# The tail of an attention and top-8 MLP kernel: full-height gather matmuls, bf16 broadcasts, one tile's statistics on ScalarE, other wait and hint places

## The chip, the cores and the metric

The kernel runs on one core of a Trainium2 chip. Its engines are TensorE (PE in the profile; its weight loads are PEld), VectorE (DVE), ScalarE (ACT), GpSimd (POOL) and SyncE (SP), which issues most of the DMAs. Each engine has its own in-order instruction stream, and they meet through semaphores. The metric is device time in microseconds, the median over several executions.

## The reference

For x of 2048 rows by 448 columns, in bf16:

```
h  = x + Attn(layernorm(x))          # 16 heads of 28 columns, one K and one V for all heads
n  = layernorm(h)
r  = n @ w_r                         # one score per row
idx = the 8 rows with the largest r
y  = ((silu(n[idx] @ w_gate) * (n[idx] @ w_up)) @ w_down) * sigmoid(r[idx])
out = h + n, with y added to the 8 rows idx
```

The gate and up matrices are 448 by 1792, the down matrix 1792 by 448. Only 8 rows go through the MLP, but which 8 they are is known only when r of all 2048 rows is known.

## The kernel before, in words

**Planner.** The kernel describes its work as a list of operations, each with its engine, an estimated duration, the keys that it reads and writes, and a priority (`_Graph.op`). `plan` simulates the five engines with these estimates and picks, whenever an engine is free, the ready operation with the lowest priority number. What comes out is a fixed order for each engine. `finish` works out which semaphore waits remain, and `emit` (L217) writes the instructions: of the waits of one instruction, the last in the list is carried by the instruction itself, and those ahead of it become waits of their own in front of it; a DMA gets all of them in front.

**Attention.** The work is 16 blocks: block b takes head group b % 4 (4 heads) and query quarter b // 4 (512 queries). A block goes over 16 key tiles of 128 keys. For most tiles ScalarE takes the exponential of two 128x1024 score tiles (`act_unit`, L884); for three to five of them VectorE builds it by integer arithmetic (`dve_unit`, L896, and `shift`, L902). TensorE multiplies the result with V into an accumulator bank. After a block (`post_block`) the sums are inverted and the block's output is scaled, on POOL and by way of DRAM; for the last block, b = 15, this is done at once on VectorE and ScalarE: a shuffle that copies the row sums to all rows (L640), a clamp (L642), Ln and Exp as reciprocal (L646, L648), each in two halves of 256 columns, and four products of 128 columns (L652).

**The last four row tiles.** Tiles 0 to 11 are projected, normalised and written out during the attention. For tiles 12 to 15 `last_pre` accumulates the first three head groups and the residual in PSUM banks 3 to 6 beforehand. What follows block 15 is one dependent chain, the tail:

- `last_proj` adds the fourth head group (one matmul per tile) and takes mean and variance of each tile on VectorE (L810, L811).
- `last_ln` takes 1/sqrt(variance) by Ln and Exp on ScalarE (L816, L818), forms r of the 512 rows on VectorE (L820 to L827; L827 writes it to a spare column of `x_sb`), and has ScalarE write the normalised rows `xn` (L836). The reciprocals `Li` of the last block's row sums (L662) stand in VectorE's order among these; they only feed a range flag.
- r is turned into a row by four matmuls (L1010), and VectorE finds the 8 largest of 8 earlier candidates and 512 new values (L1012, L1013).
- The 8 positions are cast to f32 (L1015) and broadcast to all 128 partitions by an f32 matmul with a 1-row column of ones (L1021). Comparing them with a row index gives one-hot columns `oh5` (L1023): four blocks of 128 rows for the tiles, and a fifth, 8 rows high, for candidates from earlier tiles, whose rows lie in `xnc` and `extc` (8 partitions).
- The weights 1/(1+exp(-r)) are computed (L1016 to L1020) and broadcast by a second f32 matmul (L1027, copied out by L1029).
- The gather (L1036 to L1041): for each of four column chunks, four matmuls with 128 rows and one with 8 rows pick the 8 rows of n into `xselT` (L1042). Five small matmuls give the row numbers for the scatter (L1054 to L1059).
- Gate and up projections are 56 matmuls each (L1066); silu is Exp, Ln, Exp on ScalarE, the first reading PSUM (L1071), then three VectorE products (L1074 to L1079), in two halves.
- `row_mm` (L1044) gathers h + n of the 8 rows by the same 4 + 1 matmuls per chunk, into the banks in which the 56 down-projection matmuls (L1084) then accumulate. The sum is copied out (L1088), transposed back, cast (L1093, L1095), and scattered to 8 rows of the output by an indirect DMA on POOL (L1096).

**Branch at the end.** Each engine reads the range flag (L1141) and branches (L1152) past a second, exact version of the kernel that follows in its stream; a branch hint instruction (L1137) stands in the middle of each engine's order. SP then waits for the output DMAs (L1168).

Nearly all tensors are touched through two helpers: matmuls have L371 (in the changed kernel L383), DMA issues of SP L385.

## Time and profile before

| | |
|---|---|
| median of 3 runs | 404.59 us (404.42 to 405.1) |
| profiled execution: its own time | 403.72 us |
| profiled execution: span of the core | 401.9 us |
| ScalarE busy | 375.6 us (93%) |
| VectorE busy | 354.8 us (88%) |
| TensorE busy | 348.9 us (87%) |
| GpSimd busy | 62.2 us (15%) |
| last ScalarE exponential of the attention ends | 377.87 us |
| last instruction that computes (scatter issue on POOL) ends | 399.07 us |

The span is the time from the first to the last instruction in the trace; the execution's own time contains in addition what lies around it. Busy shares are averages over the whole span; the tail is the last 24 us of it and has its own limits, so it is read by the timeline, instruction by instruction. A timeline row gives start, length, engine, line, operation, tile names and sizes, the number of merged instructions, and in brackets how long the engine had been idle and who released it.

### The profile page before, as it was taken

Reading aid. Unit: us, or ns where it says so; the run is one execution under the profiler, and the core shown is the slowest. Engines: PE = TensorE matmul, PEld = TensorE weight load, DVE = VectorE, ACT = ScalarE, POOL = GpSimd, SP = SyncE. Lnnn points to the kernel's source line nnn. Section 1 sums busy time; section 2 is a strip of 40 time slices with the busy share of each in tenths; the row PEclk is TensorE's granted clock in tenths of the full one; section 3 lists DMA queues with packets and bytes.
Section 4 is the critical chain, followed back from the end, with each engine's and each line's share of the span. In section 5 each row is a group of like instructions: output and inputs, shape, how many; then the busy total and the mean of one; then the engine's idle time right before and its main releaser. Section 6 shows DMA issues by size and latency. Waiting matters only on the chain.

```text
span 401.9 us, 8036 instructions
## 1 busy us (share of the span) xinstructions
PE 348.9 (87%) x3367; PEld 109.9 (27%) x3367; DVE 354.8 (88%) x577; ACT 375.6 (93%) x423; POOL 62.2 (15%) x111
## 2 busy tenths in 40 slices
PE   7899889898897989989898989899898989789854
PEld 7333222222222222222222222222222222222244
DVE  6995799998899999898999899998989999999361
ACT  4999999999999999999999999999999999999761
POOL 8240001211001021101011111111020121206000
PEclk9999999999999999999999999999999999999955
DMA  7694000100010010110001000200001110111010
GB/s 195 175 246 148 1 2 3 56 3 27 2 31 0 6 48 3 42 36 27 25 29 47 22 31 5 72 2 29 27 27 47 44 44 19 49 46 32 1 43 14
DMA packets 18078, 17.14 MB, mean 43 GB/s; under 512 B 6684, under 2 KB 15156, under 8 KB 18036
## 3 DMA queue, kind: packets, MB, share of 16 engines
q1 hardware_dynamic: 17940, 16.55, 14.1%
q8 instruction: 27, 0.44, 0.5%
q14 instruction: 15, 0.12, 0.1%
q0 software_dynamic: 96, 0.03, 0.1%
HBM read 11.71 MB, written 4.86 MB: 41 GB/s over the span
## 4 chain that ended last, share of the span: by engine, by line
ACT 62%; PE 17%; DVE 17%; POOL 1%; issue 1%; DMA 1%; SPq 1%; POOLq 0%; DVEq 0%
ACT P L884 61%; PE ps L371 17%; DVE Y L896 7%; DVE Y L902 5%; DMA wv_sb<-in_A_wv_dram 1%; POOL hbuf L702 1%; SPq L385 1%; DVE Ot L658 1%; DVE bn L810 1%; DVE junk L710 0%; DVE hbuf L696 0%; DVE x_sb L708 0%; DVE Q L488 0%; DVE wo_pad L784 0%; DVE bn L698 0%
## 5 line engine op out<-in xcount | busy, mean ns | idle before, releaser
L884 ACT ACTIVATE P<-ps 128x1024 bf16<-128x1024 f32 x390 | 361.9, 1083 | 5.1 <-PE ps L371 3.9
L371 PE MATMUL ps<-Q,K 64*128 64x512 bf16 x1024 | 180.7, 384 | 35.9 <-ACT P L884 27.8
L896 DVE TENSOR_SCALAR Y<-ps 128x1024 int16<-128x1024 f32 x122 | 148.1, 1214 | 15.3 <-PE ps L371 15.1
L902 DVE TENSOR_SCALAR Y<-Y 128x2048 int16<-128x2048 int16 x122 | 119.1, 976 | 2.1
L371 PEld LDWEIGHTS ps<-Q,K 64*128 64x128 bf16 x1024 | 44.5, 93 | 179.1 <-ACT P L884 143.3
L371 PE MATMUL ps<-Y,Vs 128*32 128x512 bf16 x976 | 84.8, 383 | 2.9 <-DVE Y L902 2.9
L371 PE MATMUL ps<-P,Vs 128*32 128x512 bf16 x780 | 77.2, 388 | 0.0
L670 POOL TENSOR_TENSOR Ls<-Ls,Lc 128x16 f32<-128x16 f32 x15 | 9.9, 661 | 188.7 <-DMA Lc<-h_scr 188.7
L371 PEld LDWEIGHTS ps<-Y,Vs 128*32 128x32 bf16 x976 | 24.6, 95 | 32.4 <-issue 16.8
L371 PEld LDWEIGHTS ps<-P,Vs 128*32 128x32 bf16 x780 | 19.8, 93 | 43.2 <-issue 42.1
L674 POOL TENSOR_TENSOR On<-Ot,Rb 128x512 bf16<-128x512 f32 x15 | 19.2, 1283 | 76.7 <-DMA Rb<-h_scr 76.7
L371 PE MATMUL ps<-xnT,wq_pad 112*128 112x512 bf16 (+1 forms) x68 | 19.4, 371 | 0.4 <-DVE Ot L658 0.2
L371 PE MATMUL ps<-wo_pad,On 128*128 128x448 bf16 (+1 forms) x64 | 17.2, 358 | 1.5 <-DVE On L652 1.5
L702 POOL TENSOR_TENSOR hbuf<-st,nhalf 128x1 f32<-128x1 f32 x12 | 9.5, 791 | 20.2 <-DVE st L700 20.2
L488 DVE TENSOR_SCALAR Q<-ps,qone 128x512 bf16<-128x512 f32 x15 | 10.8, 717 | 1.1 <-PE ps L371 1.1
L658 DVE COPY Ot<-ps 128x512 f32<-128x512 f32 x15 | 10.2, 680 | 0.0
L710 DVE SCALAR_TENSOR_TENSOR junk<-hbuf,w_rb 128x448 bf16<-128x448 f32 x12 | 8.1, 677 | 0.0
L696 DVE TENSOR_TENSOR hbuf<-ps,x_sb 128x448 f32<-128x448 f32 x12 | 7.4, 618 | 0.8 <-PE ps L371 0.8
L371 PE MATMUL ps<-ident 128*128 128x128 bf16 x72 | 6.2, 253 | 1.8 <-POOL ident L400 1.8
L698 DVE BATCH_NORM_STATS2 bn<-hbuf 128x6 f32<-128x448 f32 x12 | 7.4, 617 | 0.1
L589 DVE BATCH_NORM_STATS2 bn<-x_sb 128x6 f32<-128x448 bf16 x12 | 7.0, 604 | 0.0
L371 PEld LDWEIGHTS ps<-wo_pad,On 128*128 128x128 bf16 x64 | 4.2, 97 | 9.5 <-issue 5.8
(185 smaller groups left out, 162.0 us busy)
## 6 DMA issues: line engine op xcount, KB each, us to landing
Rb<-h_scr SPq DMA_DIRECT2D x15, 256.0 KB
h_scr<-hbuf SPq DMA_DIRECT2D x12, 225.0 KB, 2.4
out_dram<-x_sb SPq DMA_DIRECT2D x8, 224.0 KB, 2.2
wg_sb<-in_B_w_gate_dram SPq DMA_DIRECT2D x1, 1568.0 KB, 11.4
wu_sb<-in_B_w_up_dram SPq DMA_DIRECT2D x1, 1568.0 KB, 17.7
wd_sb<-in_B_w_down_dram SPq DMA_DIRECT2D x1, 1568.0 KB, 21.0
x_sb<-in_A_x_dram SPq DMA_DIRECT2D x3, 448.0 KB, 5.6
x_sb<-in_A_x_dram SPq DMA_DIRECT2D x4, 112.0 KB, 2.3
```

The lines of the kernel that those rows point to most:

```text
L371: return lambda e: e.matmul(o, lhsT=l, rhs=r, start=start, stop=stop)
L488: G.op(DV, lambda e: e.tensor_scalar(Q[:, b % 4, :], ps[:, bank, :], qone[:, 0:1], None, ALU.add), dvt(512), reads=[pk(bank), "qone"], wri ...
L658: G.op(DV, lambda e: e.tensor_copy(Ot[:, rb, :], ps[:, acc_bank(b), :]), dvt(512), reads=[pk(acc_bank(b))], writes=[("Ot", rb)], prio=u - 30)
L670: G.op(LE, lambda e: e.tensor_tensor(Ls[:, :], Ls[:, :], Lc[:, rb, :], ALU.add), 150, reads=["Ls", ("Lc", rb)], writes=["Ls"])
L674: G.op(PO, lambda e: e.tensor_tensor(On[:, qb % 2, g, :], Ot[:, rb, :], Rb[:, rb, :], ALU.mult), 1270, reads=[("Ot", rb), ("Rb", rb)], wri ...
L696: G.op(DV, lambda e: e.tensor_tensor(h, ps[:, bank, 0:D], x_sb[:, t, 0:D], ALU.add), dvt(D), reads=[pk(bank), ("x", t)], writes=[("h", hr)])
L698: G.op(DV, lambda e: e.bn_stats(bn6[:, t, :], h), dvt(D), reads=[("h", hr)], writes=[("bn6", t)])
L702: G.op(PO, lambda e: e.tensor_tensor(s4, st[:, t, 7:8], nhalf[:, 0:1], ALU.pow), 570, reads=[("st7", t), "nhalf"], writes=[("h4", hr)])
L710: G.op(DV, lambda e: e.scalar_tensor_tensor(junk[:, :], h, s4, w_rb[:, :], ALU.mult, ALU.mult, accum_out=st[:, t, 2:3]), 700, reads=[("h", ...
L884: G.op(AC, lambda e: e.activation(P[:, sl, :, :], ps[:, b0:b0 + 2, :], ACT.Exp, bias=EBIAS, scale=OCT), 905, reads=[pk(b0), pk(b0 + 1)], w ...
L896: G.op(DV, lambda e: e.tensor_scalar(Y[:, n, 0, p:p + 3:2, :].bitcast(I16), ps[:, 4:6, :], 0.0, 32639.0 - 3 * STEP, ALU.max, ALU.min), 114 ...
L902: G.op(DV, lambda e: e.tensor_scalar(Y[:, n, v:2 * v, :, :].bitcast(I16), Y[:, n, 0:v, :, :].bitcast(I16), v * STEP, None, ALU.add), 70 + ...
```

## The change

The list below follows the diff from top to bottom.

1. **Waits sorted.** `emit` sorts an instruction's waits by the time at which the planner expects them to be met, latest last. `op` gets an argument `after`, an order without a semaphore.
2. **Full height.** `extc` and `xnc` become 128 partitions high; the region is cleared once by POOL (`clear_ext`), which the built order places on POOL between the sixth `Ls` and the sixth `Lsi`. The fifth matmul of each gather then has 128 rows.
3. **Constants.** POOL fills a bf16 128x128 tile of ones and a cleared bf16 128x5x8 tile `bz` at the start.
4. **Last block.** The halves are taken one after the other: shuffle, clamp, shuffle, clamp on VectorE; Ln, Exp, Ln, Exp on ScalarE.
5. **Statistics.** Tile 12's mean and variance come from two ScalarE passes over PSUM with summed outputs (Identity, then Square about the mean) and one small VectorE scaling; the three other tiles stay on VectorE. In the built order the flag's `Li`, `Ls` come after the three `ra` operations, and `Lsi` after r.
6. **Position broadcast.** The positions are split in two bf16 terms (a cast and a subtraction) in row 0 of `bz` and broadcast by two bf16 matmuls of 128 rows.
7. **Weights.** They are computed later (ScalarE takes their Exp after the fourth `xn`), split in three bf16 terms by four more VectorE operations, and broadcast by three bf16 matmuls into bank 7; in the built order these stand between the gate and the up projection.
8. **Silu.** VectorE first copies the gate to SBUF, clamped at -43, for each half; the Exp reads that copy.
9. **Hints.** On POOL and SP the branch hint stands first in the order, ahead of SP's first load. VectorE's flag load moves, in the built order, from behind `idxc` to between the last `guT` product and the copy `yT`.

```diff
     def op(self, eng, fns, dur, reads=(), ..., form=0,
+           after=()):
...
+        for p in after:
+            need(p, p.eng != eng)
...
+    def met(self, wait):
+        key, v = wait
+        o = self.ops[key[1]] if isinstance(key, tuple) else self.orders[key][v - 1]
+        return o.end + o.lat
...
-            for key, v in self.waits[o.idx].items():
+            for key, v in sorted(self.waits[o.idx].items(), key=self.met):
...
-    extc = xnF[0:8, 3072:3072 + XW + 16]
-    xnc = xnF[0:8, 3584:3584 + D + 16]
+    extc = xnF[:, 3072:3072 + XW + 16]
+    xnc = xnF[:, 3584:3584 + D + 16]
...
+    G.op(PO, lambda e: e.memset(onesb[:, :], 1.0), 200, writes=["onesb"])
+    G.op(PO, lambda e: e.memset(bz[:, :, :], 0.0), 100, writes=["bz"])
...
+    def clear_ext():
+        G.op(PO, lambda e: e.memset(xnF[:, 3072:4096], 0.0), 1100, writes=xk(1))
...
+        if k == 0:
+            G.op(AC, lambda e: e.activation(hbuf[:, 0, 0:D], ps[:, bank, 0:D], ACT.Identity, scale=1.0 / D,
+                                            accum_out=mv[:, t, 0:1]), 650, reads=[pk(bank)], writes=[("h", 0), ("mv0", t)])
+            G.op(AC, lambda e: e.activation(hbuf[:, 0, 0:D], ps[:, bank, 0:D], ACT.Square, bias=mv[:, t, 0:1],
+                                            scale=-1.0, accum_out=sq[:, 0:1]), 650,
+                 reads=[pk(bank), ("mv0", t)], writes=[("h", 0), "sq"])
+            G.op(DV, lambda e: e.tensor_scalar(mv[:, t, 1:2], sq[:, 0:1], 1.0 / D, None, ALU.mult), 70,
+                 reads=["sq", ("mv0", t)], writes=[("mv", t)], prio=301)
+            return
...
-    G.op(DV, lambda e: e.tensor_copy(posf[:, 1, :], idx8[:, 1, :]), 90, ...)
-    G.op(PE, mm(ps[:, 2, 0:8], ones1[:, :], posf[:, 1, :], True, True), 100, ...)
+    G.op(DV, lambda e: e.tensor_copy(bz[0:1, 0, :], idx8[:, 1, :]), 90, reads=[("idx8", 1), "bz"], writes=["bz0"])
+    G.op(DV, lambda e: e.tensor_tensor(bz[0:1, 1, :], idx8[:, 1, :], bz[0:1, 0, :], ALU.subtract), 90, ...)
+    G.op(PE, [mm(ps[:, 2, 0:8], onesb[:, :], bz[:, i, :], i == 0, i == 1) for i in range(2)], 60, ...)
...
-    G.op(PE, mm(ps[:, 2, 8:16], ones1[:, :], wrow[:, :], True, True), 100, reads=["ones1", "wrow"],
-         writes=[pk(2)], prio=310.5)
...
-        fns.append(mm(psg[:, ch, :], xnc[:, ch * CK:ch * CK + 128], oh5[0:8, 4, :], False, True))
+        fns.append(mm(psg[:, ch, :], xnc[:, ch * CK:ch * CK + 128], oh5[:, 4, :], False, True))
...
+    G.op(PE, [mm(ps[:, 7, 64:72], onesb[:, :], bz[:, i, :], i == 2, i == 4) for i in range(2, 5)], 90,
+         reads=["onesb", "bz", "bz2", "bz3", "bz4"], writes=[pk(7)], prio=321.5)
...
-        fns.append(mm(psy[:, ch, :], extc[:, ch * CK:ch * CK + 128], oh5[0:8, 4, :], False, False))
+        fns.append(mm(psy[:, ch, :], extc[:, ch * CK:ch * CK + 128], oh5[:, 4, :], False, False))
...
+        G.op(DV, lambda e, sl=sl, bg=bg: e.tensor_scalar(eg[:, sl, :], pgu[:, bg, :, :], -43.0, None, ALU.max), 130, ...)
...
-                at = {lst[len(lst) // 2].idx: [hint]}
+                at = {lst[0 if eng in (PO, SP) else len(lst) // 2].idx: [hint]}
```

More of the change, by code (lines that the diff above doesn't have):

```diff
@@ L1014, in _main @@
          writes=[("idx8", 1)])
-    G.op(DV, lambda e: e.tensor_copy(posf[:, 1, :], idx8[:, 1, :]), 90, reads=[("idx8", 1)], writes=[("posf", 1)])
-    G.op(AC, lambda e: e.activation(wrow[:, :], top8[:, 1, :], ACT.Exp, scale=-1.0), 200, reads=[("top8", 1)],
-         writes=["wrow"])
-    G.op(DV, lambda e: e.tensor_scalar(wrow[:, :], wrow[:, :], 1.0, None, ALU.add), 70, reads=["wrow"],
-         writes=["wrow"], prio=311)
-    G.op(DV, lambda e: e.reciprocal(wrow[:, :], wrow[:, :]), 100, reads=["wrow"], writes=["wrow"], prio=311)
-    G.op(PE, mm(ps[:, 2, 0:8], ones1[:, :], posf[:, 1, :], True, True), 100, reads=["ones1", ("posf", 1)],
-         writes=[pk(2)])
+    G.op(DV, lambda e: e.tensor_copy(bz[0:1, 0, :], idx8[:, 1, :]), 90, reads=[("idx8", 1), "bz"], writes=["bz0"])
+    G.op(DV, lambda e: e.tensor_tensor(bz[0:1, 1, :], idx8[:, 1, :], bz[0:1, 0, :], ALU.subtract), 90,
+         reads=[("idx8", 1), "bz0"], writes=["bz1"])
+    G.op(PE, [mm(ps[:, 2, 0:8], onesb[:, :], bz[:, i, :], i == 0, i == 1) for i in range(2)], 60,
+         reads=["onesb", "bz", "bz0", "bz1"], writes=[pk(2)])
     G.op(DV, lambda e: e.tensor_tensor(
@@ L1026, in _main @@
         writes=["oh5"])
-    G.op(PE, mm(ps[:, 2, 8:16], ones1[:, :], wrow[:, :], True, True), 100, reads=["ones1", "wrow"],
-         writes=[pk(2)], prio=310.5)
-    G.op(DV, lambda e: e.tensor_copy(wbc[:, :], ps[:, 2, 8:16]), 70, reads=[pk(2)], writes=["wbc"], prio=330)
+    G.prio = 321
+    G.op(AC, lambda e: e.activation(wrow[:, :], top8[:, 1, :], ACT.Exp, scale=-1.0), 200, reads=[("top8", 1)],
+         writes=["wrow"])
+    G.op(DV, lambda e: e.tensor_scalar(wrow[:, :], wrow[:, :], 1.0, None, ALU.add), 70, reads=["wrow"],
+         writes=["wrow"])
+    G.op(DV, lambda e: e.reciprocal(wrow[:, :], wrow[:, :]), 100, reads=["wrow"], writes=["wrow"])
+    G.op(DV, lambda e: e.tensor_copy(bz[0:1, 2, :], wrow[:, :]), 90, reads=["wrow", "bz"], writes=["bz2"])
+    G.op(DV, lambda e: e.tensor_tensor(wlo[:, :], wrow[:, :], bz[0:1, 2, :], ALU.subtract), 90, reads=["wrow", "bz2"],
+         writes=["wlo"])
+    G.op(DV, lambda e: e.tensor_copy(bz[0:1, 3, :], wlo[:, :]), 90, reads=["wlo", "bz"], writes=["bz3"])
+    G.op(DV, lambda e: e.tensor_tensor(bz[0:1, 4, :], wlo[:, :], bz[0:1, 3, :], ALU.subtract), 90, reads=["wlo", "bz3"],
+         writes=["bz4"])
     for k in range(4):
```

45 lines of the change are left out of this document (28 added, 17 removed).

## Prediction

> **What bounds the kernel now.** I read the page first (slices, chain, groups), then the timeline of the last 24 us, instruction by instruction.
>
> ```profile
> span 401.9 us, 8036 instructions
> PEclk9999999999999999999999999999999999999955
> ACT 62%; PE 17%; DVE 17%; POOL 1%; issue 1%; DMA 1%; SPq 1%; POOLq 0%; DVEq 0%
> L884 ACT ACTIVATE P<-ps 128x1024 bf16<-128x1024 f32 x390 | 361.9, 1083 | 5.1 <-PE ps L371 3.9
> ```
>
> ScalarE carries the chain: 390 exponentials, 361.9 of 401.9 us, with 5.1 us idle before them in all. The instruction order of the attention is the same in both kernels apart from one POOL memset and the hints, so that part keeps its time. Behind them comes the tail, where no engine is full and one dependent chain sets the end. The granted clock is 0.5 in the last two slices (381.8 on), so the matmul rows from there on are at that clock already.
>
> The tail's timeline (start, length, engine, line):
>
> ```profile
> 379.31 0.48 DVE L642 TENSOR_SCALAR Ot<-Ot 128x256 f32<-128x256 f32 x2
> 380.25 0.70 ACT L648 ACTIVATE Rb<-Rb 128x256 f32<-128x256 f32 x2
> 380.68 0.88 DVE L652 TENSOR_TENSOR On<-ps,Rb 128x128 bf16<-128x128 f32 x4 [0.89 <-ACT Rb L648]
> 381.51 0.32 SPq L385 DMA_DIRECT2D Lc<-h_scr  x1
> 382.64 0.60 DVE L810 BATCH_NORM_STATS2 bn<-ps 128x6 f32<-128x448 f32 x1
> 383.23 0.60 DVE L810 BATCH_NORM_STATS2 bn<-ps 128x6 f32<-128x448 f32 x1
> 383.87 0.17 DVE L811 BATCH_NORM_AGGREGATE mv<-bn 128x2 f32<-128x6 f32 x1
> 384.63 0.18 DVE L827 TENSOR_TENSOR x_sb<-ra,st 128x4 bf16<-128x4 f32 x1
> 384.90 1.96 ACT L836 ACTIVATE xn<-ps,st 128x448 bf16<-128x448 f32 x3 [0.37 <-DVE st L829]
> 386.75 0.19 ACT L1016 ACTIVATE wrow<-top 1x8 f32<-1x8 f32 x1
> 387.01 0.16 DVE L1015 CAST posf<-idx 1x8 f32<-1x8 uint32 x1
> 387.09 0.15 DVE L1018 TENSOR_SCALAR wrow<-wrow 1x8 f32<-1x8 f32 x1
> 387.22 0.59 PE L371 MATMUL ps<-posf,ones 1*128 1x8 f32 x2 [1.74 <-DVE posf L1015]
> 387.28 0.19 DVE L1020 RECIPROCAL wrow<-wrow 1x8 f32<-1x8 f32 x1
> 387.85 0.20 DVE L1023 TENSOR_TENSOR oh<-iota_n,ps 128x40 bf16<-128x40 f32 x1 [0.38 <-PE ps L371]
> 388.10 0.59 PE L371 MATMUL ps<-wrow,ones 1*128 1x8 f32 x2 [0.29 <-DVE oh L1023]
> 388.62 0.27 PE L371 MATMUL ps<-oh,xn 128*128 128x8 bf16 x4
> 388.82 0.18 PE L371 MATMUL ps<-oh,xnT 8*128 8x8 bf16 x1
> 389.88 0.24 PE L371 MATMUL ps<-x_sb,oh 128*8 128x2 bf16 x4
> 389.99 0.19 DVE L1042 CAST xselT<-ps 112x32 bf16<-112x32 f32 x1 [1.10 <-PE ps L371]
> 390.32 1.64 PE L371 MATMUL ps<-xselT,wg_sb 112*128 112x8 bf16 x56
> 391.82 1.63 PE L371 MATMUL ps<-xselT,wu_sb 112*128 112x8 bf16 x56
> 393.31 0.25 PE L371 MATMUL ps<-oh,x_sb 128*128 128x8 bf16 x4
> 393.56 0.22 DVE L1079 TENSOR_TENSOR guT<-ps,sg 128x56 bf16<-128x56 f32 x1 [0.16 <-PE ps L371]
> 394.56 1.65 PE L371 MATMUL ps<-guT,wd_sb 128*128 128x8 bf16 x56
> 396.25 0.19 DVE L1088 CAST yT<-ps 112x32 bf16<-112x32 f32 x1 [2.47 <-PE ps L371]
> 398.14 0.93 POOL L1096 DMA_INDIRECT out_dram<-wq_sb,idxc  x1 [27.03 <-DVE wq_sb L1095]
> ```
>
> The reader is to see three things. VectorE takes one statistic after another, 0.60 us apart, and the chain to r (384.63) hangs on the last one's end, 384.04. The second f32 broadcast (388.10) stands on TensorE between `oh5` (387.85) and the gather (388.62), though the gather doesn't need it. And the 20 matmuls of a gather take 388.62 to 389.88, 1.26 us, while 56 matmuls of the same 8 columns take 390.32 to 391.82, 27 ns each. In a gather the four full-height matmuls and the 8-row one alternate: 0.20 us from the first of four to the 8-row one (388.62 to 388.82; at 27 ns it would be 0.11), so 0.115 from there to the next four (1.26/4 - 0.20).
>
> **The change part by part.**
>
> *Halves one after the other (A).* Clamp h0 no longer waits for the second shuffle: Ln, Exp and the products of half 0 come about 0.4 us sooner. But the second half's shuffle starts later, behind the first clamp, and its Ln behind the first Exp: its Exp ends at 380.95 now (380.25 + 0.70) and by my estimate at 381.0. The last product comes out about where it was; I take -0.05, with 0.2 either way (one of four products, 0.88/4).
>
> *Tile 12 on ScalarE (A).* One of four statistics leaves VectorE: 0.60 (382.64 to 383.23). In its place stands a small scaling that must wait for two ScalarE passes. They start about when the second Exp ends, 380.9 (ScalarE overlaps its instructions by 0.1); three `xn` passes of the same size take 1.96, 0.62 apart and 0.72 long. Two dependent passes with accumulator reads, unseen in this trace, I put at 0.8 each: done at 382.5. VectorE reaches the scaling at about 383.2. Cover 0.7; were a pass 1.2 us, nothing would be left. The last aggregate moves from 383.87 to 383.22, and r, 0.76 behind it, from 384.63 to 384.0. The `Li` reciprocal now stands ahead of r's last operation and waits for the `Lc` load. That load is issued after both clamps, about 0.27 later (381.78), and lands 1.7 later (row below), 383.5; VectorE gets there at 383.7. Part A: -0.62, between -0.8 and 0.
>
> *Positions in bf16 (B).* Now: cast at 387.01, `oh5` at 387.85, 0.84. After: cast, dependent subtraction (pitch of two dependent small operations 0.19, 387.09 to 387.28), end of the second 0.16 later, PE 0.05 later, two bf16 matmuls about 0.30 (the gather's last matmul starts 0.115 before 389.88, and VectorE follows at 389.99, 0.22 later; one more, and the load): 0.70. -0.14, between -0.35 (no extra pitch) and +0.2 (broadcast no faster than f32). In VectorE's order the weight's addition waits for ScalarE's Exp ahead of `oh5`, and that Exp now comes after four `xn`: (384.90 - 0.62) + 4 x 0.61 + 0.19 = 386.91, against `oh5` at 387.08. It just fits.
>
> *Second broadcast out of the way (C).* 388.10 to 388.62: -0.52. The four VectorE operations that split the weights (0.19 pitch) fit between `oh5` and `xselT`. Its three matmuls, now between gate and up, add 3 x 27 ns = +0.08 (F); their input is ready more than 1 us before. VectorE's clamp of the gate puts 0.25 into the silu chain (0.22 as L1079 of that size, and a hand-over). Its last product ends at 393.78 now, and only the second half of the down projection needs it, 394.56 + 0.82: cover 1.6, of which the shorter `row_mm` (G) takes 0.7 and the clamp 0.25. ScalarE's four output tiles, 0.61 each, end at about 389.4, when the gate's first half is done (388.3 + 0.8 and its way through PSUM).
>
> *Full-height gathers (D, G).* 20 matmuls at 27 ns are 0.54: -0.72 for 388.62 to 389.88, and -0.71 for 393.31 to 394.56. Both lie on the path: `xselT` waits for the first, the down projection follows the second on TensorE. Bounds: all of it, or nothing if what slows them isn't the height. From `xselT` to the gate the 8-row matmul of the row numbers goes as well: 0.33 becomes 0.24, -0.09 (E).
>
> The Trainium skill, "TensorEngine Tiling (Array Packing)", section Key Properties, says that a change of the tiling mode drains the array; the trace agrees with it by the 0.20 and 0.115 us above. Against the change speaks "TensorE: Matmul & The Clock Gate", Part 2, step 1, in the same skill: load time scales with columns, and the row count doesn't matter; by that alone full height would bring nothing (rival 3).
>
> *Waits, hints, end (H, I).* The last scatter's waits become ScalarE, VectorE, then the two output DMAs, long met: two more wait instructions after the last event. A hint costs 50 ns (row below), and I take the same for a wait: +0.1, between 0 and +0.2. SP's hint ahead of the first load moves everything by +0.05. VectorE's flag load (0.54) now stands before `yT`, with 1.5 us of cover (2.47 idle ahead of L1088 now, less 0.71 and 0.25).
>
> ```profile
> Lc<-h_scr SPq DMA_DIRECT2D x16, 8.0 KB, 1.7
> L1137 SPq BRANCH_PREFETCH_HINT  x1: 50/50/50, 200.1 to 200.1; - x1
> L1141 DVEq TENSOR_LOAD <-flag x1: 541/541/541, 390.4 to 390.4; - x1
> out_dram<-wq_sb,idxc POOLq DMA_INDIRECT x1, 2.7
> L1152 POOLq COMPARE_BRANCH  x1: 75/75/75, 398.4 to 398.4; - x1
> L1108 SPq DRAIN  x1: 13/13/13, 401.1 to 401.1; - x1
> L1108 POOLq DRAIN  x1: 383/383/383, 401.3 to 401.3; - x1
> ```
>
> *Sum:* A -0.62, B -0.14, C -0.52, D -0.72, E -0.09, F +0.08, G -0.71, H +0.10, I +0.05: **-2.57 us**. Against the profiled execution's span of 401.9 that is 399.3, and against its own time of 403.72 it is 401.15. That execution lies 0.87 under the median of the runs shown, 404.59; on the median the forecast is **402.0**.
>
> **The rivals.**
>
> 1. *The hint also shortens POOL's end.* POOL branches at 398.4, but its closing drain starts at 401.3, 2.8 us later, after SP's at 401.1 and just before the span ends. If POOL is waiting for code there, a hint given at the start may bring it sooner, and the end is SP's: up to -0.45 (the drain's end, 401.3 + 0.38, against SP's, 401.1, less a hop). For it: nothing else on POOL is recorded behind the scatter's issue, which ends at 399.07. Against it: the scatter itself lands only at 400.84 (398.14 + 2.7), and a drain may wait for it. 401.6.
>
> 2. *The POOL memset holds up the attention.* It has half the size of `wq_pad`'s (1.79 us), so 0.9 us, and falls among VectorE's shifts.
>
> ```profile
> L418 POOL MEMSET wq_pad<- x1: 1794/1794/1794, 1.7 to 1.7; 128x2048 bf16 x1
> L902 DVE TENSOR_SCALAR Y<-Y x122: 629/1186/2191, 41.6 to 372.3; 128x2048 int16<-128x2048 int16 x61, 128x4096 int16<-128x4096 int16 x61
> ```
>
> The longest shift took 2.19 where the median row of its kind is about 1.2, so it can be held for about 1 us. If ScalarE then starves for the whole memset, +0.9: 402.9. Against it: VectorE has slack in the attention (88% busy), ScalarE's chain doesn't pass through the shifts. The Trainium skill's "SBUF — State Buffer", Who interferes with whom, says that VectorE in its two-port modes and GpSimd lock each other out for a whole instruction; the 2.19 fits it.
>
> 3. *Height isn't what slows the gathers.* Then D, E and G are void: 402.0 + 1.5 = 403.5. For it: an alternation of tiles and an accumulation group's end fall on the same matmul. Against it: the gate's groups end after every fourth matmul without a loss.
>
> 4. *Slower: the hint holds up SP ahead of the first load.* If SP must fetch the hinted code before it goes on, and then its own again, everything shifts. The nearest row for such a fetch is POOL's 2.8 us; once gives 404.8 (no change), twice 407.6. It decides from 3.4 us on. Against it: the five hints of this trace take about 50 ns each, in the middle of running streams.
>
> **How the numbers follow.** Chances: forecast 0.54, rival 1 0.18, rival 2 0.05, a partial loss in A (an `Lc` load or a ScalarE pass that is late, up to all of A, 402.6) 0.05, rival 3 0.06, rival 4 0.12, of which 0.05 end within 0.2% of the time before (0.8 us, about what a measurement can tell from no change). The likeliest one's own range is 401.5 to 403.1 (A, B and H at their ends). The range, which leaves out rival 4 and some of the others' ends, is 401.0 (rival 1 with A, B and H at their best) to 403.7 (rival 3 with H and part of B at their worst). Faster by over 0.2%: 0.88 from the cases above, less 0.05 for a mechanism that I don't see: 0.83; same 0.06; slower 0.11.
>
> **What would show it.** Right: 20 matmuls of each gather in 0.55 us; three `bn` rows on VectorE and r near 384.0; `xselT` near 388.1; gate at 388.3; down projection near 391.9; scatter near 395.6. Wrong: VectorE idle before the scaling or before `Li`; gathers still over 1 us; a gap on SP before its first load, or a first exponential more than 0.1 later than in the trace before; a ScalarE gap of 1 us soon after the sixth `Ls`.

## The result and the profile after

The changed kernel takes 401.34 us (median of 19 runs, 399.76 to 403.79), the kernel before 403.81 (median of 19 runs, 402.21 to 405.1). The ratio of the two is put at 0.9944, with a 95% interval of 0.9930 to 0.9957: 2.26 us less (the medians themselves lie 2.47 us apart). In two later comparisons the same kernel gave 0.9931 (0.9912 to 0.9950) and 0.9917 (0.9901 to 0.9933). The profiled execution is the fastest of the 19, 399.76 us with a span of 397.9, while that of the kernel before, 403.72, was near its median: the two spans differ by more than the kernels do.

From the page of the changed kernel, the lines that answer to those of the kernel before:

```profile
span 397.9 us, 8051 instructions
PEclk9999999999999999999999999999999999999975
L913 ACT ACTIVATE P<-ps 128x1024 bf16<-128x1024 f32 x390 | 361.7, 1088 | 4.2 <-PE ps L383 2.9
```

ScalarE still carries the attention, with the same 390 exponentials and 361.7 us of work. What changed is behind them, in the tail's timeline (start, length, engine, line; in brackets the idle time before and who ended it):

```profile
380.03 0.49 DVE L668 TENSOR_TENSOR On<-ps,Rb 128x128 bf16<-128x128 f32 x2 [0.26 <-ACT Rb L664]
380.03 0.54 ACT L831 ACTIVATE hbuf<-ps 128x448 f32<-128x448 f32 x1
380.44 1.15 DVE L839 BATCH_NORM_STATS2 bn<-ps 128x6 f32<-128x448 f32 x2
380.47 0.19 ACT L831 ACTIVATION_READ_ACCUMULATOR hbuf<-ps 128x1 f32 x1
380.69 0.63 ACT L833 ACTIVATE hbuf<-ps,mv 128x448 f32<-128x448 f32 x1
381.23 0.19 ACT L833 ACTIVATION_READ_ACCUMULATOR hbuf<-ps,mv 128x1 f32 x1
381.58 0.60 DVE L839 BATCH_NORM_STATS2 bn<-ps 128x6 f32<-128x448 f32 x1
382.18 0.12 DVE L836 TENSOR_SCALAR mv<-sq 128x1 f32<-128x1 f32 x1
382.22 0.18 DVE L840 BATCH_NORM_AGGREGATE mv<-bn 128x2 f32<-128x6 f32 x1
383.01 0.17 DVE L856 TENSOR_TENSOR x_sb<-ra,st 128x4 bf16<-128x4 f32 x1
383.66 0.70 DVE L1042 MAX8 top<-ps 1x8 f32<-1x520 f32 x1
385.19 0.16 DVE L1045 CAST bz<-idx 1x8 bf16<-1x8 uint32 x1
385.59 0.21 PE L383 MATMUL ps<-bz,onesb 128*128 128x8 bf16 x2 [1.64 <-DVE bz L1046]
385.96 0.16 DVE L1057 TENSOR_SCALAR wrow<-wrow 1x8 f32<-1x8 f32 x1 [0.42 <-ACT wrow L1055]
386.04 0.18 DVE L1050 TENSOR_TENSOR oh<-iota_n,ps 128x40 bf16<-128x40 f32 x1
386.27 0.27 PE L383 MATMUL ps<-oh,xn 128*128 128x8 bf16 x4 [0.47 <-DVE oh L1050]
386.42 0.25 PE L383 MATMUL ps<-oh,xn 128*128 128x8 bf16 x4
386.89 0.24 PE L383 MATMUL ps<-x_sb,oh 128*8 128x2 bf16 x4
387.00 0.19 DVE L1078 CAST xselT<-ps 112x32 bf16<-112x32 f32 x1
390.34 0.25 PE L383 MATMUL ps<-oh,x_sb 128*128 128x8 bf16 x4
390.87 1.64 PE L383 MATMUL ps<-guT,wd_sb 128*128 128x8 bf16 x56
392.54 0.19 DVE L1130 CAST yT<-ps 112x32 bf16<-112x32 f32 x1 [1.74 <-PE ps L383]
393.17 0.35 ACT L1135 ACTIVATE wq_sb<-ps 8x224 bf16<-8x224 f32 x1 [3.17 <-PE ps L383]
393.36 0.38 DVE L1137 CAST wq_sb<-ps 8x224 bf16<-8x224 f32 x1 [0.63 <-PE ps L383]
394.69 0.93 POOL L1138 DMA_INDIRECT out_dram<-wq_sb,idxc  x1 [24.19 <-DVE wq_sb L1137]
```

The reader is to see that a group of five matmuls of the gather now starts 0.15 us after the one before it (386.27, 386.42; before it was 1.26/4 = 0.32), that nothing stands between `oh5` (386.04) and the gather (386.27), and that VectorE idles 0.42 us ahead of the weights' addition, L1057, although the next operation in its order, `oh5`, doesn't use the weights.

The end, from the instructions of the closing code (L1150) and of the branch (L1194), by engine, with duration in ns and start:

```profile
L1194 POOLq COMPARE_BRANCH  x1: 78/78/78, 395.0 to 395.0; - x1
L1150 POOLq DRAIN  x1: 2122/2122/2122, 395.5 to 395.5; - x1
L1150 SPq DRAIN  x1: 13/13/13, 397.7 to 397.7; - x1
```

POOL's drain now starts 0.5 us behind POOL's branch, not 2.8, and lasts 2.1 us instead of 0.4. It ends at 397.62, close behind SP's closing branch (397.53), which comes when the output DMAs are done; so it seems to wait for the scatter as SP does. SP's drain is followed by the span's end after 0.2 us; before, there were 0.8 us.

Where the time of the tail went, as distances between the starts of such rows, in us (the first row begins at the end of the last exponential):

| stretch | before | after |
|---|---|---|
| last exponential, last `On` product | 3.41 | 3.41 |
| last `On` product, last aggregate | 2.59 | 1.98 |
| last aggregate, r | 0.75 | 0.79 |
| r, search of the 8 largest | 0.85 | 0.65 |
| search, cast of the positions | 1.53 | 1.53 |
| cast, `oh5` | 0.84 | 0.85 |
| `oh5`, gather | 0.77 | 0.23 |
| gather, `xselT` | 1.37 | 0.73 |
| `xselT`, gate | 0.34 | 0.25 |
| gate, up | 1.50 | 1.59 |
| up, `row_mm` | 1.49 | 1.49 |
| `row_mm`, down projection | 1.24 | 0.53 |
| down projection, `yT` | 1.69 | 1.67 |
| `yT`, scatter | 1.89 | 2.15 |
| scatter, end of the span | 3.76 | 3.25 |
| **whole tail** | **24.02** | **21.11** |

The tail is 2.91 us shorter. Ahead of it, SP's first load starts at 0.85 us instead of 0.73, the first exponential at 11.28 instead of 11.35, and the attention, first to last exponential, takes 365.55 us instead of 366.53. So about 1 us of the 3.96 by which the two spans differ lies in the attention.

### The profile page after: what moved, and what is told of

The parts are those of the page before. It is cut to its first block, busy times and chain, and to the rows that moved or that the text cites. A ratio compares the mean times of both kernels' runs of the same rounds, so it can differ in the third digit from the quotient of the medians.

```text
span 397.9 us, 8051 instructions
## 1 busy us (share of the span) xinstructions
PE 347.1 (87%) x3368; PEld 108.2 (27%) x3368; DVE 354.4 (89%) x583; ACT 377.1 (95%) x427; POOL 65.8 (17%) x114
## 4 chain that ended last, share of the span: by engine, by line
ACT 65%; PE 18%; DVE 14%; issue 1%; POOL 1%; POOLq 0%
ACT P L913 63%; PE ps L383 18%; DVE Y L925 6%; DVE Y L931 5%; ACT xn L865 1%; DVE Ot L674 1%; DVE bn L839 0%; POOL hbuf L718 0%; DVE Q L502 0%; DVE junk L726 0%; ACT K L563 0%; ACT Rb L664 0%; ACT Rb L662 0%; POOL out_dram L1138 0%; ACT wq_pad L437 0%
## 5 line engine op out<-in xcount | busy, mean ns | idle before, releaser
L913 ACT ACTIVATE P<-ps 128x1024 bf16<-128x1024 f32 x390 | 361.7, 1088 | 4.2 <-PE ps L383 2.9
L686 POOL TENSOR_TENSOR Ls<-Ls,Lc 128x16 f32<-128x16 f32 x15 | 10.7, 714 | 188.0 <-DMA Lc<-h_scr 188.0
```

The source lines that it names most:

```text
L686: G.op(LE, lambda e: e.tensor_tensor(Ls[:, :], Ls[:, :], Lc[:, rb, :], ALU.add), 150, reads=["Ls", ("Lc", rb)], writes=["Ls"])
L913: G.op(AC, lambda e: e.activation(P[:, sl, :, :], ps[:, b0:b0 + 2, :], ACT.Exp, bias=EBIAS, scale=OCT), 905, reads=[pk(b0), pk(b0 + 1)], w ...
```

## The experiments

The theory to test: each stretch of the table is shortened by the part of the change that the prediction names for it, and what lies ahead of the tail (the attention, the memset) is unchanged. The rivals are given run by run. Most stretches repeat from one execution to the next within 0.02 us, so a step is judged by its own stretch. Four don't: r to search, cast to `oh5`, the second gather and the end. The totals of one kernel's runs in one comparison spread by 0.8 to 4 us.

**The hints back in the middle** (the changed kernel otherwise).

```diff
-                at = {lst[0 if eng in (PO, SP) else len(lst) // 2].idx: [hint]}
+                at = {lst[len(lst) // 2].idx: [hint]}
```

> The changed kernel with the branch hints of POOL and SP back in the middle of their orders; nothing else. In the changed kernel POOL's closing drain starts 0.5 us after its branch, in the kernel before 2.85 us after it. Theory 1 (POOL has to fetch the code behind the branch, and the early hint has it fetched in time): here the drain starts about 2.8 us after the branch again, and the end of the span, counted from the yT copy, comes 0.4 to 0.5 us later than in the changed kernel; SP's first load starts at 0.73 instead of 0.86 us; all in all +0.3 us against the changed kernel. Rival (the place of the hint does nothing, the drain came sooner because the code behind the branch lies elsewhere): drain 0.5 us after the branch as in the changed kernel, time -0.1 us against it.

Measured: 402.06 us, ratio to the kernel before 0.9951 (0.9937 to 0.9966). The closing code and the branch:

```profile
L1194 POOLq COMPARE_BRANCH  x1: 75/75/75, 400.4 to 400.4; - x1
L1150 SPq DRAIN  x1: 13/13/13, 403.0 to 403.0; - x1
L1150 POOLq DRAIN  x1: 384/384/384, 403.1 to 403.1; - x1
```

POOL's drain starts 2.75 us behind the branch again, is then short (384 ns), and ends last. SP's first load is back at 0.74 us. So the hint's place makes both effects. This execution's attention took 369.63 us, 2.5 us of it lost in the first 39 exponentials. Its granted clock was 0.50 from 17.9 to 24.8 us, where every other profile has 1.0.

**The hint alone, on the kernel before.** The same line in the other direction.

> The kernel before with one edit: the hints of the coming branch stand first in POOL's and SP's lists instead of in the middle. Theory (the closing code of POOL is what the branch waits for, and an early hint has it there): POOL's closing drain starts about 0.5 us behind its branch instead of 2.85 us, SP's drain ends last, and from the scatter's issue to the span's end there is about 0.5 us less; SP's first load starts about 0.13 us later, so some 0.35 us remain of it in the total, 403.4 us beside 403.8. Rival (the shorter end in the profile after came from other edits of the change): the drain stays near 2.8 us and the time is that of the kernel before, or 0.1 us above it.

Measured: the drain starts 0.51 us behind the branch, SP's drain 0.23 us before the end, the first load at 0.84; but the total is 403.87 us, 1.0005 of the kernel before (0.9993 to 1.0016). The scatter took longer in this execution (SP's closing branch 3.08 us behind the scatter's issue; 2.81 in the kernel before).

**POOL's hint alone.** The first of the two runs is built on the changed kernel, not on the kernel before as its expectation says:

```diff
-                at = {lst[0 if eng in (PO, SP) else len(lst) // 2].idx: [hint]}
+                at = {lst[0 if eng == PO else len(lst) // 2].idx: [hint]}
```

> The kernel before with POOL's hint alone put first; SP's stays in the middle, so that the first load isn't moved. The profile of the kernel before with both hints first had SP's drain 0.23 us before the span's end instead of 0.77, and yet its total was 1.0005 of the kernel before. Theory 1 (the end is 0.54 us shorter and it was the chance of that sample): 0.54 us less, 403.3 us, a ratio near 0.9987. Theory 2 (what the hint saves at the end is given back where the profile doesn't show it): the same gap of 0.23 us in the profile and a ratio of 1.000 again.

Measured, for what it was: 401.14 us, beside 400.93 for the changed kernel in the same comparison. Drain 0.51 us behind the branch and first load at 0.74: POOL's hint does the one, SP's the other, and SP's buys nothing. The second run is the one meant, the same edit on the kernel before:

> The kernel before with one line altered: POOL's hint stands first, SP's stays in the middle. (The run before it with POOL's hint alone was built on the changed kernel, not on the kernel before as its expectation says, so the question of that expectation is still open; this run takes it up.) Theory 1 (the end is 0.54 us shorter, and the ratio of 1.0005 with both hints was the chance of that sample): SP's drain 0.23 us before the span's end, a ratio near 0.9987. Theory 2 (what the hint saves at the end is given back where the profile doesn't show it): the same 0.23 us and a ratio of 1.000 again, with 0.9987 outside its interval.

Measured: 0.23 us again from SP's drain to the end, and 403.71 us, a ratio of 0.9999 (0.9985 to 1.0012). That interval holds both 0.9987 and 1.000. In the four profiles with POOL's hint in the middle SP's closing branch comes 2.73 to 2.86 us behind the scatter's issue, in the ten with the hint first 2.81 to 3.08, so some 0.1 us of the 0.54 may be given back there. Whether the rest reaches the total is open; the run with both hints first speaks against all of it (0.54 less 0.12 for the first load would be 0.9990, outside its interval).

**Waits as before** (the changed kernel otherwise).

```diff
-            for key, v in sorted(self.waits[o.idx].items(), key=self.met):
+            for key, v in list(self.waits[o.idx].items()):
```

> The changed kernel without the sorting of waits. From the yT copy to the scatter's start it is 1.89 us in the kernel before and 2.15 in the changed one. Theory (the compiled order of a DMA's waits is the reverse of the order in which they are written, so sorting with the latest last puts the latest first, and the two long met waits on output DMAs come behind VectorE's): 1.89 us here, all in all -0.2 us against the changed kernel, and nothing elsewhere. Rival 1 (the 0.26 us come from something else, such as POOL's longer program): 2.15 us here, no change. Rival 2 (the sorting speeds up the attention, where VectorE's waits were reordered): the attention, from the first to the last exponential, gets longer by more than the 1 us by which two executions differ.

Measured: 401.89 us, ratio 0.9947 (0.9932 to 0.9962), beside 0.9944, 0.9931 and 0.9917 for the changed kernel: the total doesn't show the 0.2 us less that was expected. The stretch does. From the timeline of the run with the waits as before:

```profile
393.86 0.19 DVE L1130 CAST yT<-ps 112x32 bf16<-112x32 f32 x1 [1.74 <-PE ps L383]
394.49 0.35 ACT L1135 ACTIVATE wq_sb<-ps 8x224 bf16<-8x224 f32 x1 [3.16 <-PE ps L383]
395.75 0.93 POOL L1138 DMA_INDIRECT out_dram<-wq_sb,idxc  x1 [24.05 <-DVE wq_sb L1137]
```

From `yT` to the scatter it is 1.89 us, against 2.15 in the changed kernel (392.54, 394.69 above). The instructions that POOL has in front of the scatter show why. First the changed kernel's wait instructions and its load of the flag, then those of this run (durations in ns; of two, the shortest, the median and the longest):

```profile
L239 POOLq EVENT_SEMAPHORE  x2: 17/30/43, 393.6 to 393.8; - x2
L1183 POOLq TENSOR_LOAD <-flag x1: 511/511/511, 394.4 to 394.4; - x1
```

```profile
L239 POOLq EVENT_SEMAPHORE  x2: 17/1371/2725, 392.1 to 392.2; - x2
L1183 POOLq TENSOR_LOAD <-flag x1: 515/515/515, 395.5 to 395.5; - x1
```

In both, two wait instructions stand first, then POOL's flag load, and the scatter carries one wait itself (so, other than the description of the planner says, not all waits of this DMA come out in front). The flag load starts 0.63 us behind the end of the last wait instruction, and the scatter 0.25 behind that start, in all fourteen profiles. By the semaphores that the trace lists with these instructions, the last wait instruction of this run is for ScalarE's half of the cast, which ends at 394.84, and the wait for VectorE's half is the scatter's own. Sorted, the last wait instruction is for VectorE's half, which ends at 393.74, 0.22 us after ScalarE's; the two waits for output DMAs share that instruction and the scatter. So the 0.63 and 0.25 us used to start with the end of ScalarE's cast and now start with that of VectorE's. That makes 0.22 us, and the wait instruction itself ends 0.04 us later behind its cast (0.08 instead of 0.04). The two waits for output DMAs, long met, add nothing that shows.

The flag load itself stands in this chain in both kernels. An earlier indirect DMA on POOL, which has no load in front, starts 0.19 us behind its last wait instruction in the kernel before (366.48) and 0.16 in the changed one (366.17). By that, moving the flag load out of the changed kernel's chain would be worth about 0.7 us (0.88 less these); this is an estimate, and no run tried it.

The same run has 0.34 us from `xselT` to the gate, not 0.25:

```profile
388.25 0.19 DVE L1078 CAST xselT<-ps 112x32 bf16<-112x32 f32 x1
388.59 1.64 PE L383 MATMUL ps<-xselT,wg_sb 112*128 112x8 bf16 x56 [0.18 <-DVE sel L1097]
```

Full height is in this kernel, so those 0.09 us come from the sort. Here, as in the kernel before, a wait instruction of 51 ns for VectorE stands ahead of the first weight load, which carries the wait for a DMA that landed long before; sorted, the weight load carries the wait for VectorE and nothing stands between.

**Full height alone, on the kernel before** (with the clearing memset).

```diff
-    extc = xnF[0:8, 3072:3072 + XW + 16]
-    xnc = xnF[0:8, 3584:3584 + D + 16]
+    extc = xnF[:, 3072:3072 + XW + 16]
+    xnc = xnF[:, 3584:3584 + D + 16]
...
-        fns.append(mm(psg[:, ch, :], xnc[:, ch * CK:ch * CK + 128], oh5[0:8, 4, :], False, True))
+        fns.append(mm(psg[:, ch, :], xnc[:, ch * CK:ch * CK + 128], oh5[:, 4, :], False, True))
```

> The kernel before with only the full-height gathers: extc and xnc 128 partitions high, cleared once by POOL, the fifth one-hot block used at full height in the two gathers and for the row numbers. Theory (each change between 8-row and 128-row matmuls costs about 0.085 us): each gather takes 0.55 to 0.62 us instead of 1.26, from oh5 to the down projection's start 1.4 to 1.5 us less, total -1.4 us. Rival 1 (another limit takes the place, VectorE's or ScalarE's chain for the down projection): the second gather is short but TensorE then waits for guT, total -0.8 us. Rival 2 (the memset holds VectorE's shifts and with them ScalarE): the attention is up to 0.9 us longer, total -0.5 us.

Measured: 402.38 us, ratio 0.9960 (0.9945 to 0.9975). Gather to `xselT` 0.73 us, `row_mm` to down 0.53, `xselT` to gate 0.34: the tail is 1.29 us shorter, all of it in the two gathers. The attention takes 366.63 us (366.53 before) with the memset in it. From the timeline of this run, the second gather:

```profile
393.00 0.25 PE L371 MATMUL ps<-oh,x_sb 128*128 128x8 bf16 x4
393.53 1.63 PE L371 MATMUL ps<-guT,wd_sb 128*128 128x8 bf16 x56
```

**8-row matmuls kept, but grouped.** The kernel before with the 16 matmuls of 128 rows of `row_mm` first and its four of 8 rows behind them: same matmuls, two changes of height instead of eight.

```diff
-        row_mm(ch, 326 + 0.1 * ch)
+        for k in range(4):
+            o = (12 + k) * XW + ch * CK
+            fns.append(mm(psy[:, ch, :], x_raw[:, o:o + 128], oh5[:, k, :], k == 0, False))
+    for ch in range(NCH):
+        fns.append(mm(psy[:, ch, :], extc[:, ch * CK:ch * CK + 128], oh5[0:8, 4, :], False, False))
```

> The kernel before with the second gather's matmuls in another order: first all 16 of 128 rows, then the four of 8 rows. Same matmuls, same sizes. Theory (what costs is the change from one height to the other): two changes instead of eight, 0.54 + 0.17 = 0.7 us for the gather instead of 1.25. Rival (an 8-row matmul costs 0.17 us more by itself): 1.25 us as before, 0.43 for the 16 and 0.8 for the four. Second rival (only the count of rows loaded matters and heights are free): 0.54.

Measured (one execution, 403.65 us): `row_mm` to the down projection 0.69 us, where it was 1.24 with eight changes and 0.53 with none.

```profile
393.84 0.57 PE L371 MATMUL ps<-oh,x_sb 128*128 128x8 bf16 x16
394.34 0.26 PE L371 MATMUL ps<-oh,xnT 8*128 8x8 bf16 x4
394.54 1.65 PE L371 MATMUL ps<-guT,wd_sb 128*128 128x8 bf16 x56
```

So it is the change of height that costs: (1.24 - 0.53)/8 = 0.089 us each in the gather, (0.69 - 0.53)/2 = 0.08 here. The small height itself costs nothing that shows. In two other profiles, the changed kernel's second and the one with the hints back in the middle, the full-height second gather took 0.67 and 0.66 us: 0.13 to 0.14 us more pass ahead of its fifth matmul, and no run shows why.

**All statistics on VectorE** (the changed kernel otherwise).

```diff
-        if k == 0:
+        if k < 0:
```

> The changed kernel with the statistics of all four tiles on VectorE: ScalarE's two accumulating passes over tile 12 are gone. Theory (the two bn operations that ScalarE took over are what shortened the stretch from the last normalised product to the last aggregate from 2.59 to 1.98 us): the stretch is 2.3 to 2.6 us, the lower end if the first pair of bn operations finds room between the two halves, and the total is 0.3 to 0.6 us above the changed kernel's. Rival (the order by halves alone made the gain): the stretch stays at 2.0 us and the total stays.

Measured: 401.97 us, ratio to the kernel before 0.9953 (0.9938 to 0.9968); the changed kernel had 401.02 in the same comparison, so the difference of 0.95 us is larger than the theory's 0.3 to 0.6. VectorE's rows:

```profile
380.71 0.49 DVE L668 TENSOR_TENSOR On<-ps,Rb 128x128 bf16<-128x128 f32 x2 [0.24 <-ACT Rb L664]
381.46 0.63 DVE L839 BATCH_NORM_STATS2 bn<-ps 128x6 f32<-128x448 f32 x1 [0.26 <-PE ps L383]
382.00 0.47 DVE L668 TENSOR_TENSOR On<-ps,Rb 128x128 bf16<-128x128 f32 x2
384.12 0.16 DVE L840 BATCH_NORM_AGGREGATE mv<-bn 128x2 f32<-128x6 f32 x1
```

One statistic slips in between the two halves, but delays the second half by 0.53 us. The stretch that the expectation names is therefore 2.06 us, as its rival has it, only because the last product, from which it counts, is late. From the first shuffle to the last aggregate it is 5.24 us, 5.25 in the kernel before, and 4.64 in the changed one. So in this order the halves alone bring nothing, and the two ScalarE passes bring all of part A. My expectation that the gap between the halves would take part of it in was wrong: the gap is 0.26 us and the operation 0.6.

**Three steps mended** (the changed kernel with VectorE's work on the weights behind `oh5` and `xselT`, a DMA's waits sorted the other way round, SP's hint in the middle).

```diff
-            for key, v in sorted(self.waits[o.idx].items(), key=self.met):
+            for key, v in sorted(self.waits[o.idx].items(), key=self.met, reverse=o.dma):
...
-         writes=["wrow"])
+         writes=["wrow"], after=[oh_op])
...
+    G.op(DV, lambda e: e.tensor_copy(bz[0:1, 3, :], wlo[:, :]), 90, reads=["wlo", "bz"], writes=["bz3"], prio=312,
+         after=[xs_op])
...
-                at = {lst[0 if eng in (PO, SP) else len(lst) // 2].idx: [hint]}
+                at = {lst[0 if eng == PO else len(lst) // 2].idx: [hint]}
```

> The changed kernel with three edits mended: VectorE's two operations on the weights stand behind oh5 and behind xselT; of a DMA's waits the one met last is written so that it comes out last in the built order; SP's hint is back in the middle, POOL's stays first. Theory (each of these three steps fell short for the cause named): from yT to the scatter 1.89 us instead of 2.15; from the positions to oh5 0.66 us instead of 0.85; SP's first load at 0.73 us instead of 0.85; together 0.5 us less than the changed kernel, about 400.8 us. Rival 1 (oh5 is not held by the weights' addition but by its own operand): 0.85 us stays and the total gains 0.35 us. Rival 2 (the weights are late for their own broadcast once they stand behind oh5): from up's first matmul on, the product with the weights waits and up to 0.3 us is lost between down and the scatter.

Measured: 401.15 us, ratio 0.9935 (0.9921 to 0.9950); the total expected was about 400.8. All three stretches came out as the theory has them. VectorE's rows:

```profile
385.93 0.16 DVE L1045 CAST bz<-idx 1x8 bf16<-1x8 uint32 x1
386.58 0.20 DVE L1050 TENSOR_TENSOR oh<-iota_n,ps 128x40 bf16<-128x40 f32 x1 [0.31 <-PE ps L383]
386.70 0.16 DVE L1057 TENSOR_SCALAR wrow<-wrow 1x8 f32<-1x8 f32 x1
```

From the cast to `oh5` it is 0.66 us; from `yT` to the scatter 1.89; the first load starts at 0.74; and the product with the weights waits for nothing new (up to `row_mm` 1.49 as before). The tail is 20.72 us.

**The changed kernel again, and both side by side.** The changed kernel unaltered, in the same comparison as the mended one, and then both once more in another.

> The changed kernel once more, unaltered, for a second profile. Theory (the attention's length varies from one execution to the next by about 1 us or more and is no work of the change): from the last exponential to the span's end 21.1 us again within 0.2 us, while from the first to the last exponential it takes another value than the 365.55 us of the first profile, 365.5 to 367. Rival (the change shortens the attention as well): 365.55 us again within 0.1 us, beside 366.5 us in the kernel before.

Measured: 401.02 us, ratio 0.9931 (0.9912 to 0.9950); tail 21.25 us, attention 365.81 us. Then:

> The mended version once more, beside the changed kernel on the same chip. Theory (the three mended steps give 0.26, 0.19 and 0.11 us, the middle one only where the granted clock falls late): 0.4 to 0.5 us less than the changed kernel in the median, and 20.7 us from the last exponential to the span's end. Rival (what the tail saves is lost in the attention's spread, or given back): the same median within 0.2 us.

> The changed kernel, unaltered, for comparison with the mended version on the same chip. Expected: a median between 401.0 and 401.4 us as in its other runs, and 21.1 to 21.3 us from the last exponential to the span's end.

Measured: mended 400.46 us, ratio 0.9905 (0.9887 to 0.9923), tail 20.86; changed kernel 400.93 us (just under the 401.0 to 401.4 expected), ratio 0.9917 (0.9901 to 0.9933), tail 21.16, attention 366.19. The mended version was 0.13 us above the changed kernel the first time and 0.47 below it the second; its tail was 0.53 and 0.30 us shorter in the profiles. From `yT` to the scatter it gains 0.26 us each time; whether it gains in the total, these runs don't settle.

The profiles also show what the granted clock does to the tail. Windows (bounds, length, busy time with count of PE, PEld, DVE, ACT and POOL, granted clock, DMA share, GB/s) of the changed kernel's second profile:

```profile
382.00:382.50 0.50, 0.00 (x0) 0.00 (x0) 0.50 (x2) 0.35 (x2) 0.00 (x0) 0.59 0.00 0
382.50:383.00 0.50, 0.00 (x0) 0.00 (x0) 0.50 (x3) 0.00 (x0) 0.00 (x0) 0.50 0.15 15
```

The same view of the changed kernel's first profile, and then one window of the kernel before:

```profile
383.00:383.50 0.50, 0.26 (x4) 0.20 (x4) 0.49 (x7) 0.22 (x1) 0.00 (x0) 1.00 0.00 0
383.50:384.00 0.50, 0.31 (x5) 0.09 (x2) 0.48 (x3) 0.50 (x2) 0.00 (x0) 0.90 0.00 0
```

```profile
383.00:383.50 0.50, 0.00 (x0) 0.00 (x0) 0.50 (x3) 0.00 (x0) 0.00 (x0) 0.97 0.00 0
```

In the second profile the clock was 0.5 before r was ready (383.94), and r to the search takes 0.85 us, as in the kernel before, whose clock fell at 383.47, ahead of r (384.63). In the first, and in the mended kernel's two, r's four matmuls still ran at 1.00, and it takes 0.65. The search then comes 0.2 us earlier, and that decides whether the weights' Exp is late for `oh5`: 0.85 us from cast to `oh5` in the first profile, 0.66 in the second.

## Why the prediction was right, and which steps were off

The forecast was a change of -2.57 us; measured, -2.26 (interval -1.74 to -2.83) in the comparison of the result. The mechanism, a dependent chain shortened part by part, is what the profiles show, but not every part came as predicted. The predicted time, 402.0, is 0.7 above the median because the three runs shown of the kernel before lay 0.8 above the 19: with 403.81 as base the same sum gives 401.24, beside 401.34. That the sum fits so well is partly luck: in the profiles its terms A to I come to -2.07, half a microsecond less than forecast, and two things that stand in no term of it, 0.20 us in r's matmuls and 0.51 at the end, make up for it. (The places that I had named, r near 384.0 to the scatter near 395.6, all lie about 1 us earlier in the profile, because the last exponential ended at 376.83 there and not at 377.87.)

- **A** (-0.62): -0.57 in the profile. Cause confirmed, with ScalarE's statistics bringing all of it. The passes took 0.54 and 0.63 us, and 0.19 each for reading the accumulator, which overlaps the pass: 0.63 and 0.73 from start to end where I had 0.8; the scaling, at 382.18, had 0.76 us of cover (I had 0.7). The halves one after the other gave 0.00 at the last product (I had -0.05).
- **B** (-0.14): +0.01. The failed step is "It just fits": the weights' Exp did not fit ahead of `oh5`. The broadcast itself was 0.18 us faster, as the mended kernel shows (0.66 from cast to `oh5`). But the faster r matmuls, which I had not foreseen, let the positions come 0.2 us sooner, while the Exp, behind four `xn` on ScalarE, ended 2.91 us behind r, just as predicted; the margin had been 0.17. Where the positions came no sooner (second profile), B gave -0.18.
- **C** (-0.52): -0.54. **F** (+0.08): +0.09. Right.
- **D** and **G** (-0.72, -0.71): -0.64 and -0.71. D fell short at its end: the last five matmuls of the first gather still take 0.20 us until the 8-column matmuls of the row numbers start (386.69 to 386.89), where the groups before take 0.13 to 0.15. Rival 3 is excluded by the two runs on height. The Trainium skill, "TensorEngine Tiling (Array Packing)", section Key Properties, has a rule that fits (a change of the tiling mode drains the array), without a price. These runs give 0.08 to 0.09 us a change. The rule of the Trainium skill in "TensorE: Matmul & The Clock Gate", Part 2, step 1, that the row count doesn't matter for the time of a weight load, agrees with the run where the 8-row matmuls are grouped, and says nothing of the changes.
- **E** (-0.09): -0.09, for a wrong reason. I put it down to the 8-row matmul of the row numbers; with full height alone the stretch stayed 0.34. It is the sorted wait.
- **H** (+0.10): +0.26. The step that failed is "two more wait instructions after the last event": POOL has two wait instructions ahead of the scatter in both kernels, and the waits for output DMAs cost nothing that shows. What costs is that the wait for VectorE's cast now stands ahead of POOL's flag load: the 0.88 us from there to the scatter start with VectorE's cast, and no longer with ScalarE's, which ends 0.22 us earlier.
- **I** (+0.05): +0.12. The hint itself takes 0.06 us in the changed kernel's trace, and about as much again passes before the load. Whether this reaches the attention can't be read: the first exponential starts at 11.28 to 12.41 us in the fourteen profiles, wherever the hint stands.
- **Rival 1** (-0.45, chance 0.18) is what happened at the end of the trace: -0.51 in the two profiles. My objection, that a drain may wait for the scatter, is true as well: the drain does wait, 2.1 us, but by its end for the same event as SP, so that POOL no longer ends after SP. The Trainium skill, "Runtime: NRT & Kernel Launch", section Instruction fetch mechanics, says that a taken branch to code outside the window stalls for a fetch. The 2.75 us without and 0.51 us with the early hint fit that, though no row shows the fetch itself. Whether this half microsecond arrives in the total could not be shown.
- **Rivals 2 and 4** did not come. The memset took 1.08 us (I had 0.9), and the attention with it 366.63 us against 366.53. SP's first load moved by 0.12 us, not by 3.

What none of the terms had: the 0.20 us of r's matmuls, which depend on when the clock drops. The prediction read 0.5 "from 381.8 on" out of a slice that is a mean of 10 us; the window above shows 0.97 for 383.0 to 383.5 in the same profile, so the clock fell 1.2 us ahead of r and not 2.8. A chain that brings r 0.57 us sooner can get ahead of the drop. In the first profile after it did, in the second it didn't; of the eight profiles with ScalarE's statistics, six have the 0.65 us.

The tail's 2.91 us less and 0.12 more at the start would be -2.8 us; the totals of three comparisons are -2.3, -2.8 and -3.4 (401.34, 401.02, 400.93 by their ratios). What lies between is the start, the end, and the attention: 365.55 to 366.19 us in three profiles of the changed kernel, 366.02 to 366.49 in five of its variants, and 366.43 to 366.63 in the five of the kernel before and its variants, one of them with the memset. Whether the changed kernel's attention is in truth some tenths shorter isn't decided; no experiment ties it to a part of the change.

## What to carry to other kernels

In a tail where one chain sets the end, count changes of matmul height, since eight of them cost more here than the 20 matmuls themselves; and take out of the chain any operation that an in-order engine waits for on behalf of someone else, as L1057 did ahead of `oh5`. When instruction order is written by a planner, look at the built order of waits for each kind of instruction: the same sort that saved 0.09 us on a matmul cost 0.26 us on a DMA, because it put the last wait ahead of 0.88 us that could have started without it. And judge edits of tenths of a microsecond by the stretch in the trace that they touch, because totals of this kernel move by 0.3 us and more from one comparison to the next.

## What was not expected of the hardware

- Ahead of the last scatter, POOL's load of one flag word starts 0.63 us behind the end of the wait instruction in front of it, in all fourteen profiles, so the order of waits decides what these 0.63 us can run beside. What fills them no row shows.
- A hint in the middle of POOL's stream did not spare the branch its 2.75 to 2.90 us; the same hint as the first instruction of the stream did (0.51 us), in all ten profiles with it there. Why the place matters was not tried.
- The granted clock falls from 1.00 to 0.50 in the tail at a moment that differs between executions of the same kernel. The trace's clock record, from which the means of 0.90 and 0.59 in the windows above are taken, has the step at 383.90 in the first profile of the changed kernel, 7.1 us behind the end of the last exponential (376.83), and at 382.09 in the second, 4.3 us behind it (377.76). The stretch at 1.00 before it began at 5.02 and 6.62 us and lasted 378.88 and 375.47: 111 and 110 times 3.413 us. In all fourteen profiles every stretch between two steps is a whole multiple of that (111 of them in twelve; 3, 2 and 106 in the run with the hints back in the middle), and the drop comes 4.3 to 7.6 us behind the last exponential. So in these runs the clock steps on a raster of 3.413 us, and where the raster lies against the tail changes from execution to execution.
